# Clustered attention with a Fourier and feed-forward layer: weight pieces joined already scaled, column sums with the images as weights, maxima spread in bfloat16

## The chip, the cores and the metric

The kernel runs on one core of one Trainium2 chip. The metric is the device time of one execution in microseconds; several runs are made, and their median counts. The profile is of one execution and has its own time.

The engines are called as in the profile: PE (TensorE, matrix products; PEld is its weight load), DVE (VectorE), ACT (ScalarE), POOL (GpSimd) and SP (SyncE, which issues the DMAs here). PSUM is the memory that PE writes its products to; SBUF holds everything else on the core.

## The reference

Inputs are q, k and v (4 batches, 8 heads, 768 tokens, 64 columns, float32), 16 centroids per head, and two weight matrices of 512 x 2048 and 2048 x 512.

```python
q_assign = argmax(q_n . c_n);  k_assign = argmax(k_n . c_n)     # nearest centroid of each token
scores = where(q_assign == k_assign, q @ k.T / 8, -1e9)
attn   = softmax(scores) @ v                                    # heads side by side: x is (4, 768, 512)
mixed  = real(fft(fft(x, axis=1), axis=2))
u      = x + mixed
un     = (u - mean(u)) / sqrt(var(u) + 1e-6)
out    = u + relu(un @ w_ch1) @ w_ch2
```

The products are made in 16-bit halves: a float32 matrix is multiplied by a power of two and split into a high half (its 16-bit rounding) and a low half (the rest), and three products of halves make one product. The weights need this too: each of w_ch1 and w_ch2 is kept on the core as a high and a low float16 matrix (`w1h`, `w1l`, `w2h`, `w2l`).

## The kernel before

**Steps.** The program is laid out in steps. A head pair (two heads of one batch; 16 pairs in all) takes six steps, one per block of 128 query tokens. In each step come, in this order: `scores` for one block of both heads (L320, L325 on PE; the row minimum on DVE, L339; the exponential on ACT, L342; its high half on ACT, L350; its low half on POOL, L351; a transposing DMA on SP, L353), then parts of the preparation of the next pair (`prep`), then `attend` for a block of two or three steps before (72 short matmuls, L371 to L373), then a part of the weights' preparation or, later, of the layer behind the attention. `Overlap.run` writes this order out. When the four pairs of a batch are done, the Fourier transform and the feed-forward layer (`up` L846, `down` L877) of that batch are laid between the steps of the next batch. The first fold of a batch for its transform is in step 31, and needs the buffer that the weights' preparation uses until then (`arena`).

PE executes in the order in which the program is written. The order on ACT, DVE, POOL and SP is set by a planner when the program is compiled, from its own estimate of when each instruction is ready; on the chip, each engine then keeps to that order and waits where something is late.

**Spreading a maximum.** `along` (L48) copies a column of 128 numbers, one for each partition, to a row that all partitions hold: one matmul with the column broadcast as weights and the identity as the moving operand, in float32, for which PE runs two matmul instructions. `scales` calls it three times for each head pair (the largest magnitudes of q, k and v), DVE then takes the maximum (L227), and a power of two is made of its exponent alone.

**The weights.** Each matrix is taken in 16 pieces of 128 x 512 elements, 32 pieces in all; eight raw buffers hold the pieces as loaded (512 KB each over 128 partitions as the profile counts, L481). The class `Weights` is a generator that is called 41 times; call i falls in step int(0.684 i), so that one or two calls come in a step, behind its other work. For call number k (from -7):

- `load`: a piece is loaded seven calls ahead of its use.
- `signs(k)` (L506, L507): for a pair of pieces ACT makes two bfloat16 images of each from the upper 16 bits of each number, one for the positive and one for the negative elements. The images hold sign, exponent and the upper mantissa bits in a form that a matmul carries exactly.
- `block(k // 4)`, once for four pieces: eight matmuls (L491) with ones as weights and an image of 512 columns as the moving operand sum the images over the partitions. DVE takes the maximum over the 512 sums (L494) and makes of its exponent a power of two `s` and its inverse (`top_power`, L58 to L61).
- `join(k)` (L515): two matmuls with plus and minus the identity as weights put both images of a piece together in PSUM, and DVE adds the lower mantissa bits from the raw piece (L519), in place in PSUM.
- `halve(k - 1)`, one call behind the joining: ACT writes the high half of the piece times `s` (L525). For an even piece DVE subtracts it from the piece times `s` (L531); for an odd piece ACT writes the whole piece times `s` to SBUF (L528) and POOL subtracts (L529).

The tiles in PSUM for all this and for `prep` and the later layer come from one pool of three buffers (`ps_f`); the scores have two of their own (`ps_big`), the attention's result one.

## Time and profile before

| | us |
|---|---|
| median of 3 runs | 1040.7 (1040.33 to 1041.58) |
| profiled execution, its own time | 1039.64 |
| its span, first to last instruction | 1037.9 |
| busy PE / DVE / ACT / POOL | 919.5 / 594.6 / 604.9 / 587.9 |
| span in which weights are prepared, about | 3 to 179 |
| first of the folds, about | 207 |

The span is 1.74 us shorter than the execution's own time. In the page's second part the span is cut into 40 slices of equal length, each digit the busy share in tenths. A row of the groups names the line, the engine and the operation, the tile written and the tiles read with their shapes, the count, and then the busy time in us and the mean duration in ns; behind the second bar stands the idle time of the engine just before these instructions and what ended it. A row of the timeline has start and duration in us. A row of the waits has the time in us, the times it occurred and the longest. A row of the windows gives for a stretch the busy us and the instructions of each engine, the clock granted to PE (1.00 is full), the busy share of the DMA engines (over 1 where packets overlap) and what they moved.

### The profile page before, as it was taken

To read this page: it belongs to the slowest core of one execution; us is meant where nothing else is said; L and a number is where in the kernel's file an instruction comes from. 1 tells how busy PE (TensorE), PEld (TensorE's weight loads), DVE (VectorE), ACT (ScalarE), POOL (GpSimd) and SP (SyncE) were. 2 spreads that over 40 slices of the span, in tenths; PEclk is the share of its full clock that TensorE was granted. 3 is DMA by queue.
4 is the path that set the end of the run, shared out by engine and by line. 5 is a ranking of instruction groups with operands and counts; after the bars stand their busy time and mean duration, and the time that the engine had idled before them with its cause. 6 is when DMAs were issued, how large, how long until landed. Compare 5 with 4: busy or idle time off the path is not lost.

```text
span 1037.9 us, 23603 instructions
## 1 busy us (share of the span) xinstructions
PE 919.5 (89%) x9416; PEld 592.4 (57%) x9416; DVE 594.6 (57%) x1276; ACT 604.9 (58%) x948; POOL 587.9 (57%) x694
## 2 busy tenths in 40 slices
PE   4686777667999999997999999997999999899998
PEld 2243444444765757554756758555757676486673
DVE  6788788778556555668556555575555423521110
ACT  5899898545756656455756747455666552252230
POOL 2457567566766756637857747448857553362230
PEclk9688878889899999998999999998999999999999
DMA  7899999877758676679677767488666551411000
GB/s 264 195 256 231 281 213 192 175 144 145 157 104 179 104 148 134 124 142 189 105 144 139 138 125 152 87 149 179 114 105 131 101 119 33 82 32 41 11 12 21
DMA packets 396239, 140.01 MB, mean 135 GB/s; under 512 B 381784, under 2 KB 381792, under 8 KB 396128
## 3 DMA queue, kind: packets, MB, share of 16 engines
q1 hardware_dynamic: 396128, 138.50, 65.2%
q8 instruction: 73, 1.20, 0.5%
q14 instruction: 38, 0.31, 0.1%
HBM read 42.52 MB, written 6.29 MB: 47 GB/s over the span
## 4 chain that ended last, share of the span: by engine, by line
PE 47%; DVE 8%; POOL 7%; DMA 7%; ACT 6%; issue 5%; SPq 0%; ACTq 0%; POOLq 0%; DVEq 0%
PE ps_f L877 19%; PE ps_f L846 17%; PE ps_big L320 4%; DMA pt<-ph 4%; POOL ph L351 3%; DMA arena<-arena 3%; DVE ps_big L339 3%; ACT ph L350 2%; PE ps_o L371 1%; PE ps_o L372 1%; PE ps_o L373 1%; ACT p L342 1%; PE ps_big L325 1%; PE ps_f L697 1%; DVE arena L626 1%
## 5 line engine op out<-in xcount | busy, mean ns | idle before, releaser
L351 POOL TENSOR_TENSOR ph<-p,ph 128x768 f16<-128x768 f32 x144 | 242.0, 1690 | 179.9 <-ACT ph L350 152.5
L846 PE MATMUL ps_f<-arena,w1h 128*128 128x256 f16 x1536 | 272.1, 277 | 24.8 <-DMA arena<-arena 15.4
L877 PE MATMUL ps_f<-w2h,arena 128*128 128x512 f16 x768 | 238.9, 379 | 0.5 <-ACT arena L855 0.5
L846 PE MATMUL ps_f<-arena,w1l 128*128 128x256 f16 x768 | 212.5, 277 | 0.0
L342 ACT ACTIVATE p<-ps_big,rmx 128x768 f32<-128x768 f32 x144 | 129.1, 900 | 128.7 <-DVE ps_big L339 119.0
L877 PEld LDWEIGHTS <-arena 128*128 128x128 f16 x1152 | 108.7, 98 | 127.2 <-issue 5.8
L846 PEld LDWEIGHTS <-w1h 128*128 128x128 f16 x1536 | 152.3, 99 | 42.3 <-issue 21.0
L856 POOL TENSOR_TENSOR arena<-arena 128x256 f16<-128x256 f32 x192 | 128.2, 678 | 74.2 <-ACT arena L855 70.9
L339 DVE TENSOR_SCALAR_CACHE_REDUCE ps_big<-ps_big,sce 128x768 f32<-128x768 f32 x144 | 141.5, 1020 | 46.7 <-PE ps_big L325 46.7
L320 PE MATMUL ps_big<-hlk,hlq 64*128 64x384 f16 x1152 | 126.2, 344 | 30.3 <-ACT p L342 17.3
L877 PE MATMUL ps_f<-w2l,arena 128*128 128x512 f16 x384 | 145.5, 379 | 0.0
L371 PE MATMUL ps_o<-v,pt 128*128 128x66 f16 x1152 | 121.4, 196 | 12.4 <-DMA pt<-p 6.4
L855 ACT ACTIVATE arena<-ps_f,wrel 128x256 f16<-128x256 f32 x192 | 90.8, 475 | 70.5 <-DVE arena L852 68.7
L852 DVE TENSOR_SCALAR arena<-ps_f,wrel 128x256 f32<-128x256 f32 x96 | 46.3, 482 | 144.6 <-POOL arena L856 82.9
L350 ACT CAST ph<-p 128x768 f16<-128x768 f32 x144 | 117.3, 831 | 15.7 <-DMA pt<-ph 15.1
L371 PEld LDWEIGHTS <-pt 128*128 128x128 f16 x1152 | 108.5, 99 | 25.7 <-issue 13.5
L372 PE MATMUL ps_o<-v,pt 128*128 128x64 f16 x1152 | 121.1, 197 | 0.0
L373 PE MATMUL ps_o<-v,pt 128*128 128x66 f16 x1152 | 120.6, 195 | 0.0
L372 PEld LDWEIGHTS <-pt 128*128 128x128 f16 x1152 | 108.9, 99 | 2.8
L373 PEld LDWEIGHTS <-pt 128*128 128x128 f16 x1152 | 109.1, 101 | 0.0
L320 PEld LDWEIGHTS <-hlq 64*128 64x128 f16 x1152 | 54.6, 98 | 90.5 <-issue 60.0
L846 PEld LDWEIGHTS <-w1l 128*128 128x128 f16 x768 | 76.1, 99 | 20.0 <-issue 10.6
(177 smaller groups left out, 1322.8 us busy)
## 6 DMA issues: line engine op xcount, KB each, us to landing
arena<-in_moe_w_ch_dram SPq DMA_DIRECT2D x32, 512.0 KB, 5.7
scr<-in_q_dram SPq DMA_DIRECT2D x16, 384.0 KB, 3.3
scr<-in_k_dram SPq DMA_DIRECT2D x16, 384.0 KB, 5.0
vst<-in_v_dram SPq DMA_DIRECT2D x16, 384.0 KB, 4.6
out_dram<-arena SPq DMA_DIRECT2D x24, 256.0 KB, 2.0
pt<-ph SPq DMA_TRANSPOSE x168, 4.1
arena<-in_cs_dram SPq DMA_DIRECT2D x12, 192.0 KB, 3.3
arena<-in_ss_dram SPq DMA_DIRECT2D x12, 192.0 KB, 3.8
```

What stands on the lines that cost most here:

```text
L320: nc.tensor.matmul(out=ps[j][:, hf, 0:SH], lhsT=hq[rows[j], a, sl], rhs=hk[rows[j], c, hs], start=(i == 0), stop=False)
L339: self.mark = nc.vector.tensor_scalar(out=ju, in0=ps[j][:, :, 0:SH], scalar1=ne, scalar2=None, op0=ALU.mult, op1=ALU.min, accum_out=m)
L342: nc.scalar.activation(x, ju, AF.Exp, bias=m, scale=-1.0)
L350: nc.scalar.copy(out=ph[:, 0], in_=p32)
L351: nc.gpsimd.tensor_tensor(out=ph[:, 1], in0=p32, in1=ph[:, 0], op=ALU.subtract)
L371: nc.tensor.matmul(out=o[:, at:at + W], lhsT=hi, rhs=v16[:, kt, 0:W], start=(kt == 0), stop=False)
L372: nc.tensor.matmul(out=o[:, at:at + D], lhsT=hi, rhs=v16[:, kt, 66:130], start=False, stop=False)
L373: nc.tensor.matmul(out=o[:, at:at + W], lhsT=lo, rhs=v16[:, kt, 0:W], start=False, stop=(kt == ST - 1))
L846: nc.tensor.matmul(out=ps.rearrange("p (t x) -> p t x", x=P), lhsT=a[:, dc, fs], rhs=c[:, :, dc], start=(i == 0), stop=(i == 11))
L855: nc.scalar.activation(hh[:, f], ps, AF.Relu, scale=rel[:, f:f + 1])
L856: nc.gpsimd.tensor_tensor(out=hl[:, f], in0=r, in1=hh[:, f], op=ALU.subtract)
L877: nc.tensor.matmul(out=ps, lhsT=a[:, f, ts], rhs=c[:, f], start=(i == 0), stop=(i == 47))
```

## The change

- `along` reads only the upper 16 bits of the column and of the identity, as bfloat16 with a stride of two: one matmul instruction instead of two. All its callers use only the exponent of what they get.
- `block`: an image of 128 columns becomes the weights and a column of ones the moving operand, so that the sums come out one to a partition, in four columns: 32 matmuls of one column. DVE takes the maximum over the four columns, `along` spreads it, and DVE takes the maximum over the 128. After `top_power`, POOL writes plus and minus the identity times `s`, in bfloat16. They are written anew for each block, where before the plain identities were written once at the start.
- `join`: with these identities the piece comes out of the two matmuls already scaled, and DVE adds the lower bits as before; for odd pieces (k % 4 of 1 or 3) it writes the result to one SBUF tile (`X32`) instead of PSUM.
- `halve`: now in the same call as the joining. ACT copies the high half without a scale; the low half is a plain subtraction, on POOL from SBUF for odd pieces and on DVE from PSUM for even ones. ACT's second copy is gone.
- The order of the calls: the images are made four pieces ahead instead of two; a block is computed at the end of the call before the first joining that needs it; there are 40 calls, spread by 0.71 steps instead of 0.684.

```diff
--- before.py
+++ after.py
@@ -45,7 +45,9 @@
 
 def along(nc, out, col, ident):
 
-    nc.tensor.matmul(out=out, lhsT=col.broadcast_to([P, P]), rhs=ident, start=True, stop=True)
+
+    top = lambda x: x.bitcast(BF16)[:, 1::2]
+    nc.tensor.matmul(out=out, lhsT=top(col).broadcast_to([P, P]), rhs=top(ident), start=True, stop=True)
 
 
 MASK = float(2.0 ** 120)
@@ -439,6 +441,7 @@
     RAW, PN = tuple(4128 * i for i in range(6)) + (29696, 33824), (24768, 40000, 44096)
     ID, TOP, MX, ONE = 28864, 29376, 29472, 29568
     X32 = 37952
+    SB = (1, 3)
     EXTRA, A2, AHEAD = 0, 9, 7
 
     def __init__(self, tc, pool, arena, psf, w1, w2, ident):
@@ -485,17 +488,20 @@
 
         nc, at = self.nc, self.arena.at
         ps = self.psf()
-        i = 0
-        for k in range(4 * g, 4 * g + 4):
-            for j in range(2):
-                nc.tensor.matmul(out=ps, lhsT=self.ones[:, 0:1].broadcast_to([P, P]), rhs=self.bits[k][:, j], start=(i == 0), stop=(i == 7))
-                i += 1
+        for c in range(4):
+            for i in range(8):
+                nc.tensor.matmul(out=ps[:, c:c + 1], lhsT=self.bits[4 * g + i // 2][:, i % 2, c * P:(c + 1) * P],
+                                 rhs=self.ones[:, 0:1], start=(i == 0), stop=(i == 7))
         mx = at(self.MX + 32 * (g % 2), [P, 1], F32)
-        nc.vector.tensor_reduce(out=mx, in_=ps, op=ALU.max, axis=AX.X)
+        nc.vector.tensor_reduce(out=mx, in_=ps[:, 0:4], op=ALU.max, axis=AX.X)
+        along(nc, ps[:, P:2 * P], mx, self.ident)
+        top = at(self.TOP + 32 * (g % 2), [P, 1], F32)
+        nc.vector.tensor_reduce(out=top, in_=ps[:, P:2 * P], op=ALU.max, axis=AX.X)
         s = self.sb.tile([P, 1], F32, name="wsc", tag="wsc", bufs=2)
-        top_power(nc, mx, ps[:, 0:1], s, self.inv[g // 4][:, g % 4:g % 4 + 1])
-        for i in range(4):
-            self.scale[4 * g + i] = s[:, 0:1]
+        top_power(nc, top, ps[:, 0:1], s, self.inv[g // 4][:, g % 4:g % 4 + 1])
+        for i in range(2):
+            nc.gpsimd.tensor_scalar(out=self.idb[:, i], in0=self.ident, scalar1=s[:, 0:1], scalar2=1.0 - 2 * i,
+                                    op0=ALU.mult, op1=ALU.mult)
 
     def signs(self, k):
 
@@ -510,25 +516,21 @@
     def join(self, k):
         nc, at = self.nc, self.arena.at
         pn = self.bits.pop(k)
-        ps = self.sum[k] = self.psf()
+        ps = self.psf()
         for i in range(2):
             nc.tensor.matmul(out=ps, lhsT=self.idb[:, i], rhs=pn[:, i], start=(i == 0), stop=(i == 1))
         raw = self.raw(k)
         rest = raw.bitcast(U32)[:, 0:2 * DM].rearrange("p (n two) -> p n two", two=2)[:, :, 1]
-        x = ps.bitcast(U32)
-        nc.vector.scalar_tensor_tensor(out=x, in0=rest, scalar=13, in1=x, op0=ALU.logical_shift_right, op1=ALU.bitwise_or)
+        x = self.sum[k] = at(self.X32, [P, DM], F32) if k % 4 in self.SB else ps
+        nc.vector.scalar_tensor_tensor(out=x.bitcast(U32), in0=rest, scalar=13, in1=ps.bitcast(U32),
+                                       op0=ALU.logical_shift_right, op1=ALU.bitwise_or)
 
     def halve(self, k):
-        nc, ps, s = self.nc, self.sum.pop(k), self.scale.pop(k)
+        nc, x = self.nc, self.sum.pop(k)
         m, i = divmod(k, 16)
         hi, lo = (t[:, i % 4, i // 4 * DM:(i // 4 + 1) * DM] if m == 0 else t[:, i] for t in (self.w1, self.w2)[m])
-        nc.scalar.activation(hi, ps, AF.Copy, scale=s)
-        if k % 2:
-            x = self.arena.at(self.X32, [P, DM], F32)
-            nc.scalar.activation(x, ps, AF.Copy, scale=s)
-            nc.gpsimd.tensor_tensor(out=lo, in0=x, in1=hi, op=ALU.subtract)
-        else:
-            nc.vector.scalar_tensor_tensor(out=lo, in0=ps, scalar=s, in1=hi, op0=ALU.mult, op1=ALU.subtract)
+        nc.scalar.copy(out=hi, in_=x)
+        (nc.gpsimd if k % 4 in self.SB else nc.vector).tensor_tensor(out=lo, in0=x, in1=hi, op=ALU.subtract)
 
     def run(self):
         nc, at = self.nc, self.arena.at
@@ -536,21 +538,18 @@
         for i in range(2):
             nc.gpsimd.memset(self.off[:, i:i + 1], -8.0 * ((896 << 4) + 32768 * i))
         self.idb = at(self.ID, [P, 2, P], BF16)
-        for i in range(2):
-            nc.gpsimd.tensor_scalar(out=self.idb[:, i], in0=self.ident, scalar1=1.0 - 2 * i, scalar2=None, op0=ALU.mult)
         self.ones = at(self.ONE, [P, 2], BF16)
         nc.gpsimd.memset(self.ones, 1.0)
-        for k in range(-self.AHEAD, 33):
+        for k in range(-self.AHEAD, 32):
             for p in self.loads(k):
                 self.load(p)
-            if k % 2 == 0 and 0 <= k + 2 < 32:
-                self.signs(k + 2)
-            if k % 4 == 0 and 0 <= k < 32:
-                self.block(k // 4)
+            if k % 2 == 0 and 0 <= k + 4 < 32:
+                self.signs(k + 4)
             if 0 <= k < 32:
                 self.join(k)
-            if k >= 1:
-                self.halve(k - 1)
+                self.halve(k)
+            if k % 4 == 3 and -1 <= k < 31:
+                self.block((k + 1) // 4)
             yield
         self.relative()
         yield
@@ -898,7 +897,7 @@
 
     STEPS0 = ((-5, 0), (-5, 0.2), (-5, 0.3), (-5, 0.4), (-4, 0.5), (-4, 2), (-3, 2), (-2, 4), (-1, 0.5))
     V0 = (-5, -2, -1)
-    W0, WD = 0, 0.684
+    W0, WD = 0, 0.71
     END = 28
     COST, KEEP, KEEP3 = 130.4, 10.5, 7.9
 
@@ -1009,7 +1008,7 @@
                 next(wgen, None)
 
         wgen = self.wts.run()
-        n = 32 + self.wts.AHEAD + 2
+        n = 32 + self.wts.AHEAD + 1
         for i in range(n):
             at(int(self.W0 + i * self.WD), 6, weights, None)
         for pr in range(NP):
```

## The prediction

> **What bounds the kernel now.** I read the page first (busy rows by slice), then the windows, to compare the stage in which the weights are prepared with a later stage, then the chain of waits.
>
> ```profile
> span 1037.9 us, 23603 instructions
> ...
> PE   4686777667999999997999999997999999899998
> ...
> DVE  6788788778556555668556555575555423521110
> ACT  5899898545756656455756747455666552252230
> ...
> PEclk9688878889899999998999999998999999999999
> DMA  7899999877758676679677767488666551411000
> ```
>
> A slice is 25.9 us. In slices 2 to 8 ACT, DVE and DMA stand high and PE low; from slice 11 on PE is at 9 nearly throughout. The windows give that contrast in numbers.
>
> ```profile
> core 0: us, PE busy (x) PEld busy (x) DVE busy (x) ACT busy (x) POOL busy (x), PEclk, DMA share, GB/s
> ...
> 30.00:180.00 150.00, 108.89 (x1202) 58.16 (x1202) 125.34 (x260) 135.76 (x177) 94.80 (x82) 0.81 1.07 232
> 300.00:420.00 120.00, 116.44 (x1329) 77.34 (x1327) 71.49 (x154) 73.09 (x114) 73.58 (x81) 1.00 0.73 140
> 540.00:660.00 120.00, 118.09 (x1303) 78.56 (x1299) 69.11 (x144) 75.86 (x122) 77.76 (x88) 1.00 0.69 132
> ```
>
> From 30 to 180 us (stage A, the weights) ACT is busy 135.76 of 150 us, 91%; DVE 84%, PE 73%, POOL 63%, the DMA share 1.07. Afterwards (stage B) PE is busy 97 to 98% and nothing else is near. So the change is priced twice: in stage A by what it takes from ACT and where PE then waits, in stage B by PE time alone. Behind stage A the chain of waits can't be followed; in stage B it passes through the spreading of the maxima (L48) six times, first and last here:
>
> ```profile
> 305.43 0.68 PE ps_f L48 x6
> ...
> 751.98 0.67 PE ps_f L48 x6
> ```
>
> **The change, part by part.**
>
> *Maxima spread in bfloat16.* Each head pair needs three spreads, today six matmul instructions (two passes each). PE in order around one such group:
>
> ```profile
> 577.18 0.38 PE L846 MATMUL ps_f<-arena,w1h 128*128 128x256 f16 x2
> 577.40 0.27 PE L846 MATMUL ps_f<-arena,w1l 128*128 128x256 f16 x1
> ...
> 577.62 0.83 PE L48 MATMUL ps_f<-ident,amx 128*128 128x128 f32 x6
> 578.39 1.15 PE L320 MATMUL ps_big<-hlk,hlq 64*128 64x384 f16 x12
> ```
>
> The group holds PE from 577.62 to 578.39, 0.77 us. In 16-bit, two 256-column matmuls take 577.40 − 577.18 = 0.22 us, so 128 columns take 0.055 and three spreads 0.17 us; the strided read of the upper halves has no row, and at double that time it would be 0.33. The chain holds 0.67 to 0.69 us per group, so each of the six gives back 0.5 us: 3.0 us. Ten of the 16 groups lie behind stage A; with all ten on the path at 0.6 us it would be 6.0, and nothing if what follows waits for something else (as it does for the four that the chain leaves out). I take 3.0, because the chain names them.
>
> *Pieces copied without the scale.* Per piece ACT now writes the high half from PSUM with the scale (L525), and for odd pieces a second full-precision copy (L528). After, it makes one plain copy, from PSUM for 16 pieces and from SBUF for 16.
>
> ```profile
> L350 ACT CAST ph<-p 128x768 f16<-128x768 f32 x144 | 117.3, 831 | 15.7 <-DMA pt<-ph 15.1
> ...
> L235 ACT ACTIVATE hlq<-scr,scp 128x768 f16<-128x768 f32 x16 | 14.9, 933 | 18.1 <-DVE scp L408 17.7
> ...
> L815 ACT CAST arena<-arena 128x512 f16<-128x512 f32 x24 | 14.2, 612 | 0.1
> ...
> L528 ACT ACTIVATE arena<-ps_f,wsc 128x512 f32<-128x512 f32 x16 | 10.9, 681 | 0.0
> L525 ACT ACTIVATE w2h<-ps_f,wsc 128x512 f16<-128x512 f32 x16 | 10.8, 681 | 1.0 <-DVE wsc L61 0.6 <-DVE ps_f L519 0.4
> L525 ACT ACTIVATE w1h<-ps_f,wsc 128x512 f16<-128x512 f32 x16 | 10.7, 680 | 8.8 <-DVE wsc L61 8.8
> ```
>
> Today: 10.7 + 10.8 + 10.9 = 32.4 us. From SBUF a plain 512-column copy is 612 ns (L815). From PSUM no plain one is shown; 768 columns with a scale from a register column take 933, plainly 831, so I take 681 − 102 = 579 ns, with 681 as the other end. After: 16 × 0.579 + 16 × 0.612 = 19.1 us; ACT loses 13.3 us (11.7 at the other end). Its 8.8 us of waiting for the scale end too; what replaces them is a wait for DVE's pass on the same piece, now a call nearer, which the other work in ACT's queue has to cover.
>
> *DVE and POOL.*
>
> ```profile
> L531 DVE SCALAR_TENSOR_TENSOR w1l<-ps_f,wsc,w1h 128x512 f16<-128x512 f32 x8 | 6.0, 745 | 3.2 <-ACT w1h L525 3.2
> ...
> L494 DVE TENSOR_REDUCE arena<-ps_f 128x1 f32<-128x512 f32 x8 | 5.5, 683 | 1.6 <-PE ps_f L491 1.6
> ...
> L816 DVE TENSOR_TENSOR arena<-arena 128x512 f16<-128x512 f32 x4 | 2.7, 684 | 0.2
> ...
> L540 POOL TENSOR_SCALAR arena<-ident 128x128 bf16<-128x128 f32 x2 | 1.1, 530 | 0.0
> ...
> L174 DVE TENSOR_REDUCE X<-ident 128x4 f32<-128x128 f32 x1 | 0.3, 277 | 0.0
> ```
>
> Eight 512-column reductions (5.5 us) become eight of 128 (0.28 each) and eight of 4 columns, for which I put between nothing and 0.28: 2.2 to 4.5 us. Sixteen subtractions fall from 0.745 to about 0.684. DVE: −2 to −4 us, its pass per piece (L519) unchanged wherever it writes. POOL gets 16 scaled identities less the two made once: 14 × 0.53 = +7.4 us. It has 55 us free in stage A, but it is in order: a scaled identity that waits for DVE's scale holds up the subtractions (L351) behind it, and SP's transposes behind those. The loads on SP are as many as before and hang on the same DVE pass. The odd pieces share one SBUF tile, so DVE's next odd pass waits for POOL's subtraction two pieces earlier; that lies two calls back, with a step's other work between, so I cost it at nothing; without that cover DVE would stand for one subtraction per odd piece.
>
> *Column sums on PE.* Eight matmuls of 512 columns become 32 of one column, each with its own weight load.
>
> ```profile
> 43.10 3.57 PE L491 MATMUL ps_f<-arena 128*128 128x512 bf16 x8 [1.58 <-DVE w1l L531]
> ...
> 49.13 0.19 PE L371 MATMUL ps_o<-v,pt 128*128 128x66 f16 x1
> 49.16 0.20 PE L372 MATMUL ps_o<-v,pt 128*128 128x64 f16 x1
> ```
>
> Matmuls of 64 to 66 columns with a fresh load each start 0.03 us apart, so 32 take about 1.0 us, or 2.0 at half clock, against 1.9 (a row below) and 3.57: −0.9 to −1.6 per block, some −9 us of PE over eight. The Trainium skill (TensorE: Matmul & The Clock Gate, Back-to-back issue gap) speaks against this: it puts a sustained load-and-matmul pair of 128 columns at about 81 ns, by which the 32 would take an estimated 2.6 us and the eight blocks add up to 5.6 us to PE, the sum rising to at most 1038.3. The 0.03 us rows decide for me.
>
> *Waits on PE.* PE's order is fixed, so the new spread inside the block stalls everything behind it until DVE has reduced, and the next piece's joining waits for the scaled identities. First and last of the eight blocks, from column sums to scale, and between them the one that took longest:
>
> ```profile
> 19.50 2.34 PE L491 MATMUL ps_f<-arena 128*128 128x512 bf16 x5
> 22.82 0.69 DVE L494 TENSOR_REDUCE arena<-ps_f 128x1 f32<-128x512 f32 x1
> 25.85 0.15 DVE L61 RECIPROCAL wsc<-winv 128x1 f32<-128x1 f32 x1
> ...
> 121.39 0.69 DVE L494 TENSOR_REDUCE arena<-ps_f 128x1 f32<-128x512 f32 x1 [1.60 <-PE ps_f L491]
> 128.97 0.15 DVE L61 RECIPROCAL wsc<-winv 128x1 f32<-128x1 f32 x1
> ...
> 157.66 1.89 PE L491 MATMUL ps_f<-arena 128*128 128x512 bf16 x8
> 160.40 0.68 DVE L494 TENSOR_REDUCE arena<-ps_f 128x1 f32<-128x512 f32 x1
> 166.05 0.15 DVE L61 RECIPROCAL wsc<-winv 128x1 f32<-128x1 f32 x1
> ```
>
> DVE begins the reduction 0.98 and 0.85 us after PE's end in the first and the last, 1.7 on the mean of all eight; from its start to the scale's end it is 3.2 and 5.8, in the longest 7.7, on the mean 4.1. So the spread costs PE about 8 × 1.7 = 13.4 us. Then the scale, and POOL's 1.06 us: some 5 us until the next joining. Calls come 1/0.71 to a step, and by that arithmetic three of the eight blocks stand in the same step as the joining behind them (blocks 0, 1, 7): 15 us. The other five have a step's scores and attention between: 31 steps end at the first fold near 207 us, so a step is 6.7 us, 73% of it PE work, 4.9 us, which covers it. New waits: 28 us. Against that go waits for a PSUM buffer, which pieces now give back sooner: nine rows, 21.6 us, largest and smallest here.
>
> ```profile
> PE ps_f L515 <- ACT arena L528: 4.5, 2, 2.7
> ...
> PE ps_f L263 <- ACT arena L528: 0.6, 1, 0.6
> ```
>
> 28 − 21.6 − 9: PE comes out about even, within the 41 us that it stands idle in stage A.
>
> **The sum.** How much of ACT's 13.3 us shortens stage A no row says: all of it, if ACT alone sets the pace; nothing, if DVE (84%) or the transfers take over. With ACT falling to about DVE's level I take 5 us. 5 + 3.0 = 8 us off the profiled execution's 1039.64 us, 1.06 below the median: 1031.6 there, 1032.7 against the median.
>
> **The rivals.**
> 1. *ACT's saving arrives whole*: 13.3 + 3.0 to 6.0, 1021 to 1024. For it: 91% in stage A. Against: DVE has 25 us of slack there, and PE's waits must indeed come out even.
> 2. *The transfers hold stage A.* Their share is 1.07 there against 0.7 later. Nothing comes from ACT, 3.0 from stage B: 1037.7. Against: few waits on PE end in a transfer.
> 3. *Slower: PE waiting at the block becomes the bound.* In-order PE stands at the spread, then at the joining; the scores behind it come late and ACT, though emptier, waits. If the 28 us replace rather than fill PE's idle time and half reaches the end: +14 − 3 = +11, and with ACT's 5 given, +6: 1046. It decides from about 1 us of lost path per block (8 × 1 = 8 us, my whole gain). For it: DVE strung the scale out over 7.7 us in one block. Longer PE gaps also keep the clock low: granted 0.81 here, and eight column sums took 3.57 us at 43 us against 1.89 at 157. The Trainium skill (same page, What's actually happening) says the array's default is throttled and activity releases it; the 0.81 against 1.00 agrees.
>
> **How the numbers follow.** About 0.2% (2 us) is what a measurement of this kernel can tell from no change. Forecast 0.42 (its own range 1028 to 1037), rival 1 0.14, rival 2 0.19 (a half of it within 0.2%), rival 3 0.25. Faster 0.42 + 0.14 + 0.10 = 0.66, same 0.09, slower 0.25. The range must take in both sides: 1022 to 1046.
>
> **What would show it.** Spreads: groups of three matmuls holding PE 0.2 us in stage B. Copies: one ACT group of about 0.58 and one of 0.61 us, ACT under 85% from 30 to 180. The first batch's fold should start some 5 us earlier. Wrong would be: PE waits on DVE's reductions and POOL's identities over 30 us, column sums well over 2 us per block, or the DMA share climbing while ACT idles.

## The result, and the profile after

The changed kernel took 1058.21 us (median of 4 runs, 1057.34 to 1059.53), against 1041.14 (4 runs, 1040.33 to 1046.44) for the kernel before: a ratio of 1.0157, with a 95% interval of 1.0128 to 1.0187. It is 17 us slower; the forecast was 8 us faster, with a range that ended at 1046.

The page of the changed kernel, profiled at 1057.34 us, whose slices are 26.4 us each:

```profile
span 1055.5 us, 23891 instructions
...
PE   2576656568699899899899999997999999999998
...
DVE  6687888786556554658556655567555333521110
ACT  5688986654566665645665747455666543342230
...
PEclk9688988778799999999899999998999999999999
DMA  7799999676957766668767876598667552321000
```

The windows (stretch, its length, then busy us and instructions of PE, PEld, DVE, ACT and POOL, the granted clock, the DMA share, GB/s):

```profile
30.00:180.00 150.00, 95.04 (x1332) 55.45 (x1351) 116.41 (x258) 120.08 (x154) 92.48 (x90) 0.80 1.01 224
300.00:420.00 120.00, 116.29 (x1296) 75.00 (x1293) 68.98 (x148) 72.12 (x113) 74.73 (x84) 1.00 0.70 134
540.00:660.00 120.00, 117.46 (x1303) 76.48 (x1301) 71.69 (x152) 73.76 (x117) 74.94 (x85) 1.00 0.74 139
```

Behind stage A nothing has changed: PE is busy 97 and 98% again. In stage A PE is busy 14 us less than before, DVE 9 and ACT 16, some of it because the work of the stage now reaches beyond 180 us. No engine has become fuller; they wait for one another. To see where, I set the start of DVE's score pass in each of the 96 steps beside that of before. Steps are counted here and below from the first scores on, as 0; the program begins five steps earlier, so that its step 31, the first fold, is step 26 here.

```
step      start before, us    shift in the changed kernel, us
   4            54.74               +8.2
  14           129.04               -2.0
  16           142.34               +0.2
  19           161.89               +2.5
  23           188.04              +10.8
  27           221.67               +8.8
  31           255.65              +19.0
  35           299.19              +16.6
  59           519.22              +16.5
  95           845.49              +18.0
```

What the first blocks lose (8.2 us at step 4) is made good again by step 14. The loss that stays comes in two places: about 9 us between steps 16 and 27, at the last two blocks of the weights and just behind them, and 8 us between steps 27 and 35 (10 by step 31), where the Fourier transform of the first batch is being prepared and the weights are already done. The waits of PE from 12 to 215 us show one of the two (us in all, times, longest), first a row of before, then those of after:

```profile
PE ps_big L320 <- DVE X L339: 12.8, 13, 2.9
```
```profile
PE ps_f L50 <- DVE arena L496: 19.1, 8, 5.6
PE ps_big L322 <- DVE X L341: 18.5, 14, 4.8
PE ps_f L521 <- POOL arena L503: 12.5, 5, 3.9
```

The first row of after is the spread inside the block, waiting for DVE's reduction; the third is the joining, waiting for the scaled identities. Neither existed before. The second, the scores' wait for DVE, was 12.8 us before. The timelines of PE and DVE at the second block (start, duration, instruction, in brackets the idle time before it and what ended it):

```profile
42.58 0.94 PE L493 MATMUL ps_f<-arena 128*128 128x1 bf16 x32
49.15 0.29 PE L50 MATMUL ps_f<-ident,arena 128*128 128x128 bf16 x1 [5.63 <-DVE arena L496]
51.19 1.03 PE L521 MATMUL ps_f<-arena 128*128 128x512 bf16 x2 [1.74 <-POOL arena L503]
```
```profile
45.60 0.95 DVE L250 TENSOR_REDUCE amx<-vst 128x1 f32<-128x768 f32 x1 [4.51 <-DMA vst<-in_v_dram]
46.47 1.01 DVE L341 TENSOR_SCALAR_CACHE_REDUCE X<-ps_big,sce 128x768 f32<-128x768 f32 x1
...
48.34 0.69 DVE L525 SCALAR_TENSOR_TENSOR arena<-arena,ps_f 128x512 uint32<-128x512 uint32 x1
48.94 0.16 DVE L496 TENSOR_REDUCE arena<-ps_f 128x1 f32<-128x4 f32 x1
```

The sums are ready at 43.52. The reduction, 0.16 us long, starts at 48.94, because it stands in DVE's queue behind an L250 that waits 4.5 us for a load of v, and behind two score passes and the joining's pass. PE, in order too, stands still for 5.6 us, then for another 1.7 until POOL has written the identities. The Trainium skill (TensorE: Matmul & The Clock Gate, Architectural detail: the array is 16× 32×32, not 1× 128×128) has DVE's queue strictly first in, first out; the 5.4 us from 43.52 to 48.94 agree.

The other place has no instruction of the change in it except one spread. What differs there is the order of DVE's queue. Before, on DVE and on SP:

```profile
220.43 1.31 DVE L626 SCALAR_TENSOR_TENSOR arena<-arena,vseq 128x768 f16<-128x768 f32 x1 [1.00 <-ACT arena L625]
221.67 1.02 DVE L339 TENSOR_SCALAR_CACHE_REDUCE ps_big<-ps_big,sce 128x768 f32<-128x768 f32 x1
```
```profile
223.25 1.30 SPq L648 DMA_TRANSPOSE arena<-arena  x1
```

After:

```profile
230.48 1.01 DVE L341 TENSOR_SCALAR_CACHE_REDUCE ps_big<-ps_big,sce 128x768 f32<-128x768 f32 x1
...
231.42 1.01 DVE L341 TENSOR_SCALAR_CACHE_REDUCE ps_big<-ps_big,sce 128x768 f32<-128x768 f32 x1
...
232.88 1.01 DVE L625 SCALAR_TENSOR_TENSOR arena<-arena,vseq 128x768 f16<-128x768 f32 x1
```
```profile
234.55 2.04 SPq L647 DMA_TRANSPOSE arena<-arena  x1
```

The low half of the second fold (L626, now L625) went ahead of the step's score passes before and goes behind them now, so the transposing DMA that needs it is issued 11.3 us later. The score passes themselves are 8.8 us late. Nobody edited these lines: the planner placed them otherwise. The same placing, this low half behind the score passes, is in the traces of e1, e2, e6 and e14 below, and these five kernels lose 7.8 to 8.8 us between steps 27 and 35; the other thirteen experiments have it ahead, as before, and lose at most 3.6 there. That this one placing makes the whole loss there was not tried by itself.

### The profile page after: what moved, and what is told of

Same layout as the page of the kernel before. It is cut to its first block, busy times and chain, and to the rows that moved or that the text cites. A ratio compares the mean times of both kernels' runs of the same rounds, so it can differ in the third digit from the quotient of the medians.

```text
span 1055.5 us, 23891 instructions
## 1 busy us (share of the span) xinstructions
PE 907.7 (86%) x9547; PEld 585.6 (55%) x9568; DVE 592.8 (56%) x1284; ACT 595.2 (56%) x932; POOL 592.2 (56%) x708
## 4 chain that ended last, share of the span: by engine, by line
PE 52%; DMA 12%; DVE 12%; ACT 8%; issue 7%; POOL 7%; SPq 1%; ACTq 0%; DVEq 0%; POOLq 0%
PE ps_f L876 20%; PE ps_f L845 17%; PE ps_big L322 6%; DMA pt<-ph 3%; POOL ph L353 3%; ACT ph L352 3%; DVE ps_big L341 3%; DMA arena<-arena 2%; PE ps_f L696 2%; DMA vst<-in_v_dram 2%; PE ps_o L373 2%; DVE X L341 2%; PE ps_o L374 2%; PE ps_o L375 2%; PE ps_big L327 1%
## 5 line engine op out<-in xcount | busy, mean ns | idle before, releaser
L322 PE MATMUL ps_big<-hlk,hlq 64*128 64x384 f16 x1152 | 132.6, 357 | 37.9 <-DVE X L341 18.5
L352 ACT CAST ph<-p 128x768 f16<-128x768 f32 x144 | 117.4, 831 | 20.6 <-DMA pt<-ph 20.1
L373 PEld LDWEIGHTS <-pt 128*128 128x128 f16 x1152 | 108.6, 99 | 23.4 <-issue 11.3
```

Of the source, the lines that this page charges most:

```text
L322: nc.tensor.matmul(out=ps[j][:, hf, 0:SH], lhsT=hq[rows[j], a, sl], rhs=hk[rows[j], c, hs], start=(i == 0), stop=False)
L352: nc.scalar.copy(out=ph[:, 0], in_=p32)
L373: nc.tensor.matmul(out=o[:, at:at + W], lhsT=hi, rhs=v16[:, kt, 0:W], start=(kt == 0), stop=False)
```

## The experiments

Two theories stood against each other at first. *Waits*: PE's two new waits in the block make the loss. *Plan*: any edit makes the planner order DVE, ACT, POOL and SP anew, also where nothing was edited, and its new order is worse. A third, *ACT*, was the forecast's: what ACT saves shortens stage A, and something else takes more. Each run is compared with runs of the kernel before on the same chip. The kernels of e9, e10, e14, e15 and e16 leave the scale out of the weights' halves (plain identities, made once), and are read for their time alone.

### One part at a time, planned freely

e1: the kernel before with the spread in bfloat16, and nothing else.

```diff
-    nc.tensor.matmul(out=out, lhsT=col.broadcast_to([P, P]), rhs=ident, start=True, stop=True)
+    top = lambda x: x.bitcast(BF16)[:, 1::2]
+    nc.tensor.matmul(out=out, lhsT=top(col).broadcast_to([P, P]), rhs=top(ident), start=True, stop=True)
```

> The kernel before with the spread in bfloat16 and nothing else. If the spread gives back what the chain of waits holds for it (six groups of 0.67 us cut to 0.17), the time falls by about 3 us, to 1038, and the groups of three hold PE about 0.2 us in the later stage. If every microsecond that it saves is given back at the next wait for a transfer or at the folds, the time stays at 1041 within 1 us. Above 1043 the spread in bfloat16 would itself be a cause of the slowdown.

Measured: 1058.54 us against 1040.08, 1.0173 [1.0146, 1.0201]. A kernel in which 48 short operations have half the matmul instructions, and nothing else is edited, lost as much as with the whole change.

e2: the changed kernel with the old column sums (ones as weights, eight matmuls of 512), so that no spread stands in the block.

```diff
-                nc.tensor.matmul(out=ps[:, c:c + 1], lhsT=self.bits[4 * g + i // 2][:, i % 2, c * P:(c + 1) * P],
-                                 rhs=self.ones[:, 0:1], start=(i == 0), stop=(i == 7))
...
+                nc.tensor.matmul(out=ps, lhsT=self.ones[:, 0:1].broadcast_to([P, P]), rhs=self.bits[k][:, j], start=(i == 0), stop=(i == 7))
...
-        along(nc, ps[:, P:2 * P], mx, self.ident)
```

> The changed kernel with the column sums as before (eight matmuls of 512 columns with ones as weights), so that nothing has to be spread inside a block; the scaled identities, the odd pieces in SBUF and the new order of the calls stay. Theory 1, PE standing at the spread (19.1 us in eight waits in the changed kernel) is most of the slowdown: the time falls by 10 us or more, to about 1046, and the waits of PE for the first reduction are gone. Theory 2, the wait for POOL's scaled identities (12.5 us there) carries it: it stays within 4 us of the changed kernel's 1058, and the wait before the joining grows. Theory 3, the new order of the queues carries it: also about 1058, with PE's waits at the block reduced but DVE and ACT waiting as long as before.

Measured: 1072.6, 1.0305 [1.0265, 1.0345]. Taking one of PE's two waits away made it 14 us slower than the changed kernel, which none of the three theories had said (1046 or 1058).

e3: the kernel before with only the new order of the calls (images four ahead, `halve` in the joining's call, the block at the end of a call, 40 calls by 0.71).

```diff
-            if k % 2 == 0 and 0 <= k + 2 < 32:
-                self.signs(k + 2)
...
+            if k % 2 == 0 and 0 <= k + 4 < 32:
+                self.signs(k + 4)
...
+            if k % 4 == 3 and -1 <= k < 31:
+                self.block((k + 1) // 4)
...
-    W0, WD = 0, 0.684
+    W0, WD = 0, 0.71
```

> The kernel before with only the order of the calls changed: images four pieces ahead, halving in the call of the joining, the block at the end of the call before, 40 calls spread by 0.71. The arithmetic is as before (plain identities, scale in the halving, old sums, float32 spread). Theory 3, the order carries the slowdown: 1050 or more. Theories 1 and 2, the new waits inside the block do: within 4 us of 1041.

Measured: 1050.61, 1.0102 [1.0067, 1.0137]; its four runs lie between 1044.55 and 1053.75.

e4: the kernel before with the new column sums, the spread in the block and the spread in bfloat16, in the old order of calls. Old joining, old copies, plain identities.

```diff
+        for c in range(4):
+            for i in range(8):
+                nc.tensor.matmul(out=ps[:, c:c + 1], lhsT=self.bits[4 * g + i // 2][:, i % 2, c * P:(c + 1) * P],
+                                 rhs=self.ones[:, 0:1], start=(i == 0), stop=(i == 7))
...
+        along(nc, ps[:, P:2 * P], mx, self.ident)
```

> The kernel before with the column sums by images as weights and the spread inside the block (and the spread in bfloat16), in the old order of the calls and with the old joining and halving, so that no joining waits for a scale. Theory 1, the stand at the spread carries the slowdown: 1050 or more, with some 15 to 20 us of waits of PE for the first reduction. Theories 2 and 3: within 4 us of 1041, although the same waits at the spread appear.

Measured: 1059.66, 1.0189 [1.0151, 1.0227]. Two single parts cost 18 and 11 us, a third with e1's 20, and the whole 17: they don't add up. If *Plan* holds, such runs tell little, since each comes with a plan of its own.

### The same parts with the order held

To take the planner out, the queues' order was fixed at compile time: each instruction of DVE, ACT, POOL and SP gets a dependency that carries order alone, no semaphore, on its predecessor in a given order.

```diff
+    for name in PLAN:
+        i = made.get(name)
...
+        if i.engine in last:
+            tc.add_manual_dep(i, last[i.engine], mybir.DependencyInfo(mybir.DependencyClass.NoSync, mybir.DependencyReason.DATA), reason="keep")
+        last[i.engine] = name
```

e5 is e1 in the order of before. e6 is the reverse: the kernel before, every instruction as it was, float32 spreads included, in the order that the planner chose for e1.

> The kernel before with the spread in bfloat16 alone, as in the first experiment, but DVE, ACT, POOL and SP keep the order of the kernel before, instruction for instruction (edges of order alone, no waits). Theory O, the spread itself is harmless and the planner's new order of the four queues cost the 18 us of the first experiment: 1037 to 1040, the 3 us of the chain's six groups showing. Theory S, the 16-bit spread itself is slow or upsets PE: 1055 or more, as in the first experiment.

> The converse: the kernel before with its float32 spread, but with DVE, ACT, POOL and SP in the order that the planner chose for the 16-bit spread of the first experiment. No instruction differs from the kernel before. Theory O: 1055 to 1061, the whole loss without any change of the work. Theory S: within 3 us of 1041.

Measured: e5 1039.45 against 1039.34, 0.9998 [0.9974, 1.0022]; e6 1061.93, 1.0197 [1.0135, 1.0259]. Counted by line and tile in the two traces, e1's order differs from before's at 247 of 1084 places on DVE, 117 of 944 on ACT, 81 of 694 on POOL and 63 of the 389 transfers on SP. That order by itself costs about 20 us (1.97%; 22.6 between the medians), and the bfloat16 spread by itself nothing that can be measured. e6 shows the second place above: its shift goes from 12.0 us at step 27 to 23.7 at step 31. It has lost in stage A too, 13.3 us by step 19, where the changed kernel has lost 2.5; by step 23 the two stand at 12.1 and 10.8. In e5 the shift is −0.9 at step 27 and +0.3 at step 31.

e7: the changed kernel with all instructions but the weights' own held in before's relative order; the planner places only the weights' ones among them. e8: e7 with the old column sums. e13: e4 held in the same way.

```diff
+        if i.name not in Kept.own and i.engine != mybir.EngineType.PE:
+            made.setdefault(str(i.engine).split(".")[1], []).append(i)
...
+        for a, b in zip(order, order[1:]):
+            tc.add_manual_dep(l[b], l[a].name, mybir.DependencyInfo(mybir.DependencyClass.NoSync, mybir.DependencyReason.DATA), reason="keep")
```

> The changed kernel, with all instructions that are not the weights' (attention, its preparation, Fourier transform, feed-forward) held in the order among themselves that they have in the kernel before; the planner places only the weights' instructions between them. Theory O, the loss of 17 us is mostly the new order of this other work: 1045 or less, and the folding stretch behind step 27 loses nothing. Theory W, the waits inside the blocks (19.1 us of PE for the first reduction, 12.5 us for the identities) carry it: 1053 or more, with these waits as long as in the changed kernel.

> As the one before, but with the column sums of the kernel before, so that no spread stands in a block (in the second experiment the planner's free order made this 1072.6). Theory O: the 32 us of the second experiment vanish, 1045 or less. Theory W: the difference to the run before shows what the spread's wait costs when the order is the same; if it is the main cost, this is 8 us or more faster than the run before, otherwise within 4 us of it.

> The fourth experiment (the kernel before with the new column sums and the spread inside the block) with the order of the other work kept. There it was 1059.7 under a free order. If PE's stand at the spread costs its 14 to 15 us by itself, in the old order of the calls too: 1050 to 1056. If the stand costs only together with the new order of the calls (halving in the call of the joining): within 4 us of 1040, and the 19 us of the fourth experiment were the planner's.

Measured: e7 1053.47, 1.0127 [1.0091, 1.0163]; e8 1054.3, 1.0134 [1.0088, 1.018]; e13 1043.5, 1.0028 [1.0006, 1.0049]. In e7 the jump between steps 27 and 31 is gone (10.9 to 11.6), but the loss at steps 19 to 23 (2.2 to 10.6) is there as in the changed kernel. So *Plan* is one part of the loss, 4.7 of the 17 us at the end, and what is left speaks for *Waits*. Among the held instructions the planner still places the weights' own anew, in these runs and in all held ones that follow; that their place costs something, too, was not excluded. PE's waits from 12 to 215 us in e7, e8 and e13, in this order:

```profile
PE ps_f L50 <- DVE arena L496: 21.8, 8, 4.8
...
PE ps_f L521 <- POOL arena L503: 14.4, 5, 5.4
```
```profile
PE ps_f L519 <- POOL arena L501: 23.9, 5, 7.6
```
```profile
PE ps_f L49 <- DVE arena L494: 23.3, 8, 4.5
```

e8 has lost the spread's wait, and the identities' has grown from 14.4 to 23.9. e13 has a wait at the spread as large as any, and pays 3 us for it.

### The two waits apart

e9 is e7 with plain identities, made once (no wait at the joining). e10 is e9 with the old column sums too (neither wait). e14 is e10 planned freely.

```diff
-        for i in range(2):
-            nc.gpsimd.tensor_scalar(out=self.idb[:, i], in0=self.ident, scalar1=s[:, 0:1], scalar2=1.0 - 2 * i,
-                                    op0=ALU.mult, op1=ALU.mult)
...
+        for i in range(2):
+            nc.gpsimd.tensor_scalar(out=self.idb[:, i], in0=self.ident, scalar1=1.0 - 2 * i, scalar2=None, op0=ALU.mult)
```

> As the run of the changed kernel with the other work's order kept (1053.5), but with plain identities, made once at the start: the scale is left out of the weights, so that no joining waits for a block. Sums, spread and powers are still made. Theory I, the joinings' wait for POOL's scaled identities (14.4 us there) is the larger part of what remains (14 us): 1047 or less. Theory P, the spread's wait (21.8 us there) or the new place of the weights' work in the queues is: 1050 or more, with the wait of PE for the first reduction as long as before.

> As the one before, and with the old column sums, so that neither a spread nor a scale can hold up PE in a block (the scale is left out of the weights). ACT's saving of 11 to 13 us stays. If the two waits together are what remains of the loss once the order is kept: 1036 to 1042. If it stays above 1047, neither wait is the cause, but the order of the calls (halving in the call of the joining, block before the next call) under the old order of the other work.

> The tenth experiment (neither spread nor scaled identities; the scale is left out of the weights; 1038.8) with the planner's order free instead of kept. If a free order costs by itself what it cost the kernel before with the 16-bit spread: 1050 to 1062, with no wait in a block at all. If the planner's order harms only where PE also stands in the block: within 4 us of 1039.

Measured: e9 1053.1 against 1040.45, 1.013 [1.0091, 1.0169]; e10 1038.77, 0.9984 [0.9959, 1.0009]; e14 1055.06, 1.0128 [1.0093, 1.0163]. Set out in a square:

```
us                            order held        planned freely
neither wait (scale left out)  e10 1038.77       e14    1055.06
both waits                     e7  1053.47       after  1058.21
```

From e10, the waits cost 15 us and the free plan 16; both together cost 19, not 31. And one wait (e8 or e9) costs as much as both. The shifts of the four profiles show where they fail to add up. Between steps 27 and 35 the free plan loses 7.8 us in the changed kernel and 7.9 in e14, with the waits as without, against 0.9 in e7. By step 27, though, e7 is late by 10.9 us, e14 by 4.4, and the changed kernel, which has both, by 8.8; and from step 35 on e7 loses 2.8 more, e14 and the changed kernel 1.2 and 1.4. In e14 PE waits for something else, 20.0 us for the scores' transfers (`oht`), where before had 0.6. Why losses at the blocks cover each other was not taken apart further.

e10 also answers *ACT*. The windows from 30 to 180 us of e10, then of e12:

```profile
30.00:180.00 150.00, 106.13 (x1202) 56.68 (x1202) 122.78 (x260) 124.80 (x160) 94.15 (x82) 0.80 1.03 231
```
```profile
30.00:180.00 150.00, 97.63 (x1073) 53.66 (x1091) 113.25 (x238) 139.88 (x188) 85.12 (x71) 0.82 0.96 209
```

In e10 ACT is busy 124.80 us instead of 135.76, with the order held and neither wait, and the time is within its interval of the old one. But e10 has the calls spread by 0.71 steps, and that this takes what ACT's saving gives was not excluded. At 0.684, e15 below (short copies) and e13 (old copies), both with the spread's wait, stand at 1.0003 and 1.0028, which their intervals don't tell apart. e12 is the opposite test: the kernel before, the other work's order held, with the high half written twice, 32 × 0.68 = 21.8 us more for ACT.

```diff
-        nc.scalar.activation(hi, ps, AF.Copy, scale=s)
+        for _ in range(2):
+            nc.scalar.activation(hi, ps, AF.Copy, scale=s)
```

> The kernel before, with the order of the other work kept, and ACT's high half of each piece written twice (the same values to the same place): 32 more ACT passes of 0.68 us, 21.8 us more in the weights' stage. If ACT sets the pace of that stage, as the forecast's 5 us assumed in part and its first rival in full, 10 to 22 us slower, 1050 to 1062. If ACT has slack there, so that the 11 us that the change takes from it could bring nothing: within 4 us of 1040.

Measured: 1055.12 against 1040.42, 1.0122 [1.0092, 1.0151]. ACT at 91% stood at an edge: 21.8 us more cost 14.7, 11 less brought nothing that can be measured.

### Where the wait at the spread costs something

e13 shows that a wait of 23 us can be nearly free in the old order of calls, and e9 that it costs 13 us in the new. Two parts of the order of calls were put back into e9, one in each of two runs: e15 spreads the calls by 0.684 steps, as before; e16 keeps 0.71 and lays the block at the start of the call of its first joining. e17 is e7, with both waits and the scale, by 0.684.

```diff
-    W0, WD = 0, 0.71
+    W0, WD = 0, 0.684
```
```diff
+            if k % 4 == 0 and 0 <= k < 32:
+                self.block(k // 4)
...
-            if k % 4 == 3 and -1 <= k < 31:
-                self.block((k + 1) // 4)
```

> The ninth experiment (plain identities, the scale left out of the weights, the spread's wait alone; 1053.1) with the calls spread by 0.684 steps as in the kernel before instead of 0.71. If the later calls made the stand at the spread dear (13 us there, 3 us in the old order of the calls): 1047 or less. If the place of the block or of the halving did: 1050 or more.

> The ninth experiment with the block moved to the start of the call of its first joining, as in the kernel before, everything else as there. If the block's place at the end of a call, where PE stands ahead of the next step's scores, made the stand dear: 1047 or less. If the timing of the calls or the halving in the joining's call did: 1050 or more.

> The seventh experiment (the changed kernel with the order of the other work kept; 1053.5) with the calls spread by 0.684 steps. If the later calls carry what remains of the loss: 1047 or less, though PE still waits some 30 us for reductions and identities. If the waits carry it wherever the calls lie: 1050 or more.

Measured: e15 1041.57 against 1040.9, 1.0003 [0.9975, 1.003]; e16 1049.51, 1.008 [1.0055, 1.0104]; e17 1050.73, 1.0089 [1.0059, 1.0119]. PE's waits in e15 and in e17:

```profile
PE ps_f L50 <- DVE arena L496: 20.1, 8, 5.0
```
```profile
PE ps_f L521 <- POOL arena L503: 19.0, 6, 6.2
PE ps_f L50 <- DVE arena L496: 18.1, 8, 4.6
```

With the calls 4% closer, 20.1 us of waiting at the spread are free (1041.57 against e9's 1053.1); the blocks then lie earlier (the last one's sums end at 155.1 us in e15, at 169.3 in e9). The wait at the joining is not free there: e17 still pays 10 us. e16 came out between its two bounds: the block's place gave back some 4 us of 13, and its interval overlaps e9's. That the last calls of the weights, at steps 19 to 23, are what arrives too late agrees with the shifts (e7 loses 8.4 us there, e15 gains 3.0), but why a later call makes the wait cost more was not isolated.

e11 tried to remove the spread's wait while keeping the scale: the block cut in two, with the spread and the scale behind the next step's scores, and four pieces in three steps, planned freely.

```diff
+        self.open[g] = ps, mx
+
+    def spread(self, g):
+        nc, at = self.nc, self.arena.at
+        ps, mx = self.open.pop(g)
...
+            at(int(i * self.WD) if g < 0 else T0 + 3 * g + (0, 1, 2, 2)[j], 6, weights, None)
+        for g in range(8):
+            at(T0 + 3 * g, 1.5, spread, g)
```

> The changed kernel with the block cut in two and the calls laid so that four pieces take three steps: the sums at the end of a step, the spread, the scale and the identities behind the scores of the next step, the first joining at the end of that step. The planner's order is free. If PE's two waits cost what the trace of the changed kernel says, they nearly vanish here (under 8 us of 31.6) and the time falls below 1050, beyond the scatter that a free order brings. If the free order decides alone, it falls anywhere from 1040 to 1070 with the waits gone all the same.

Measured: 1083.46, 1.0426 [1.0397, 1.0455]. PE's waits:

```profile
PE ps_f L526 <- POOL arena L508: 45.6, 10, 9.4
PE ps_f L493 <- ACT ac L268: 12.9, 4, 4.4
...
PE ps_f L50 <- DVE arena L530: 5.0, 3, 1.7
...
PE ps_f L50 <- DVE arena L496: 2.1, 2, 1.1
```

The wait at the spread did fall, from 19.1 to 2.1 us (L496; the 5.0 us in three waits stand before the spreads of a head pair's maxima, and end with a joining's pass). But the joining's wait for the identities went from 12.5 to 45.6 us, and PE waited at the sums for ACT, 12.9 us. The calls lie later, too: the last block's spread starts at 209.4 us, against 167.7 in the changed kernel. The construct failed, and no gain from a shorter wait at the spread can be read from it. No version here beats both kernels by more than its interval. A second buffer for the identities with an earlier block, and a better order than before's for the changed kernel, were not tried.

## Why the prediction was wrong, point by point

**A step that was missing: the order of the other work.** The prediction priced instructions, waits and transfers as if the rest of the program stood still. The planner is in the description of the kernel before, and the steps count queues that a part is moved past, but no term and no rival says that DVE, ACT, POOL and SP are ordered anew for work that nobody touched. That alone is worth about 20 us in e6, more than twice the gain that was forecast. In the changed kernel it comes with the 8 us between steps 27 and 35; holding the order takes these away and gives back 4.7 at the end (1058.21 to 1053.47), since e7 is later by step 27 and loses more behind step 35.

**The step "28 − 21.6 − 9: PE comes out about even".** This is the step that failed in the sum. Its terms were nearly right. Forecast at the spread: 13.4 us, measured 19.1; at the joining: 15, measured 12.5, in five places; together 28 against 31.6, over the 30 us that were named as a sign of being wrong. What failed is the subtraction. PE is busy 13.9 us less from 30 to 180 us and stands idle that much longer, 55 us instead of 41. The PSUM waits that ended and the PE time that was saved did not pay for the new waits: with the order held both waits cost 14.7 us (1053.47 − 1038.77), and either alone as much. Rival 3 had this mechanism, and with "half reaches the end: +14" its price; it had a chance of 0.25, and stage A looks as it says: PE stands, the scores behind it come late, ACT is emptier and waits. That the time is 1058 and not its 1046 has two reasons: neither of the gains subtracted there came (3 for the spreads, 5 for ACT), and the plan's 4.7 us stand on top.

**A term put at nothing: the calls spread by 0.71 steps.** The prediction used the spacing to find which joinings stand close behind their block, and gave it no price of its own. e9 and e15 differ in it alone (and in where the planner then lays the weights' own instructions), with 19.1 and 20.1 us of waiting at the spread, and took 1.013 and 1.0003 of the kernel before; with the joining's wait as well (e17) the closer calls still cost 10 us. So what the wait cost hung on when the calls came, which neither the sum nor rival 3 had; that the waits' price came out near rival 3's +14 is in part luck.

**"Forecast: ACT falls to DVE's level, 5 us."** The mean durations were right:

```profile
L532 ACT CAST w1h<-arena 128x512 f16<-128x512 f32 x8 | 5.0, 620 | 0.0
L532 ACT CAST w2h<-arena 128x512 f16<-128x512 f32 x8 | 4.9, 613 | 1.1 <-DVE arena L525 1.1
L532 ACT CAST w1h<-ps_f 128x512 f16<-128x512 f32 x8 | 4.6, 581 | 7.4 <-DVE ps_f L525 7.4
L532 ACT CAST w2h<-ps_f 128x512 f16<-128x512 f32 x8 | 4.6, 571 | 5.0 <-DVE ps_f L525 5.0
```

5.0 + 4.9 + 4.6 + 4.6 = 19.1 us, the very sum predicted, and ACT is at 80% in stage A, under the 85% that was named as the sign. Its waits for the scale, 9.8 us before, gave way to 13.5 for DVE's pass (the idle times in these rows), which the other work did not cover. The gain did not come: e10 has the saving without the new waits, at 1.7 us less [−4.2, +0.9]. The first fold, which was to start some 5 us earlier, starts at 217.1 us instead of 206.0. A busy share of 91% was read as a pace. Here it said that nothing may be added (e12), not that something may be won. Rival 1, the saving whole, falls with it. Rival 2's half, nothing from ACT, fits e10, but whether the transfers are what holds stage A then was not tested.

**"Spread in bfloat16, 3.0 us."** In stage B the group of three now reads, in order on PE:

```profile
643.73 0.34 PE L50 MATMUL ps_f<-ident,amx 128*128 128x128 bf16 x3
644.00 1.15 PE L322 MATMUL ps_big<-hlk,hlq 64*128 64x384 f16 x12
```

It holds PE for 0.27 us where it held 0.77, so the 0.5 per group is right, and the 0.27 lies within the 0.17 to 0.33. e5 shows what arrives: 0.9998 [0.9974, 1.0022], which just leaves out 3.0 us (0.29%). Its steps run 1.8 us ahead at step 53 and are 0.7 behind at step 59, so in its profile the gain was made and given back. What the chain of waits held for this part was an upper bound here.

**Column sums, DVE, POOL.** The block of 32 one-column matmuls took 0.94 us from 42.58 us on, as the 1.0 us of the sum had it (1.95 at most, where the images were late). The 81 ns per pair of load and matmul by the Trainium skill (TensorE: Matmul & The Clock Gate, Back-to-back issue gap), stated for 128 columns, would have made it an estimated 2.6; pairs of one column show 0.03 us each. The rows behind DVE's and POOL's terms:

```profile
L503 POOL TENSOR_SCALAR arena<-ident,wsc 128x128 bf16<-128x128 f32 x16 | 5.8, 374 | 11.4 <-DVE wsc L63 11.0 <-DVE arena L562 0.4
...
L499 DVE TENSOR_REDUCE arena<-ps_f 128x1 f32<-128x128 f32 x8 | 2.3, 287 | 1.5 <-PE ps_f L50 1.5
L496 DVE TENSOR_REDUCE arena<-ps_f 128x1 f32<-128x4 f32 x8 | 1.2, 155 | 0.0
```

The reductions are 3.5 us instead of 5.5; the sixteen identities 5.8 instead of 16 × 0.53 = 8.5. POOL, in order, stood 11.0 us for the scale, as feared. DVE's pass into the one SBUF tile of the odd pieces waited only 0.4 us, for PE, never for POOL: costing that tile at nothing was right. The granted clock in stage A, 0.80 against 0.81, hardly fell. From 180 to 255 us it was 0.75 against 0.86, though, and in stage A e7 and e9 had 0.76 and 0.77 where e15 had 0.86. Whether a lower clock is a part of the loss, as rival 3 had it, or only goes with PE's standing still, was not tested.

## What to carry to other kernels

Where a planner orders the queues, an edit comes with a new order of everything, and in e6 that was worth about 20 us where the edit itself was worth nothing: hold the order of the untouched work, or put the new order on the old kernel, before a part is given a price. A short result that an in-order PE needs at once must be judged by the queue that makes it (a 0.16 us reduction came 5.4 us late behind someone else's load), and such waits don't add up: here one cost as much as two, and with the calls 4% closer the wait at the spread alone cost nothing. ACT's busy share of 91% told what more work would cost there, not what less would bring.

## What the runs showed of the hardware that was not expected

On POOL the identity times a scale from a register column and a constant took 374 ns where the identity times a constant alone had taken 530 (twice, at 2 us), with the same shape and types; what makes the difference was not tried. PE's one-column matmuls with their own weight loads, 0.03 us apart, were as fast in the second block as the rows of 64 columns had suggested, where eight of 512 columns had taken 3.57 us. The granted clock was 0.86 from 42 to 44 us in the one profile and 0.50 from 42 to 47 in the other.
